# Top-1 routing behind windowed attention: rows kept in token order, and a table of row numbers built by one-hot matmuls

## The chip, the cores and the metric

The kernel runs on one core of a Trainium2 chip. The metric is device time in microseconds (us) for one execution of the whole program. Beside the times there is one profiled execution, which tells for every engine (PE the matrix engine, PEld its weight loads, DVE the vector engine, ACT the scalar engine, POOL the general engine, SP the one that only issues transfers) what ran when and what ended each wait.

## The reference

Two stages run one behind the other. The first is attention over 8 batches, 8 heads, 576 positions of 64 numbers, in which a query sees the positions within 32 of its own and 8 global positions, and a global query sees all. The second sends each of the 4608 tokens (512 numbers) to one of 8 experts, the one with the largest gate logit, and scales that expert's answer by its softmax weight.

```python
mask = np.abs(pos[:, None] - pos[None, :]) <= 32
mask = mask | is_global[:, None] | is_global[None, :]
attn = softmax(where(mask, q @ k.T / 8, -1e9))
x = (attn @ v).transpose(0, 2, 1, 3).reshape(4608, 512)

logits = x @ w_gate
expert_idx = np.argmax(logits, axis=1)
gate_w = softmax(logits)[arange, expert_idx]
for e in range(8):
    m = expert_idx == e
    out[m] = gate_w[m, None] * (np.maximum(x[m] @ w1[e], 0) @ w2[e])
```

The inputs are drawn once and fixed. The experts get 446, 387, 871, 515, 596, 674, 404 and 715 tokens.

## The kernel before

**Layout.** `wall` holds the weights of all experts in f16 (16 KB of each partition for one expert). Until the weights of experts 2 to 7 arrive, their place is carved up for attention: q and k in f32 and f16, v for two batches (`vb`), exponentials for two steps (`eb`), four staging buffers, and `x16b[0]`, the finished rows of even batches. `x16b[1]`, for odd batches, is a tile of the attention pool. A row is ROW = 516 words of 16 bits: 512 numbers in f16, the token number (32 bits) and the softmax weight (f32).

**The loop.** The outer loop runs over the 8 batches, the inner one over t, 6 steps a batch. A step computes the scores of the next step (`scores`, L419), their exponentials on ACT (`exps`, L443), then `pvs` (L447, 32 matmuls) and `zs` (L461, the sums of the exponentials, 32 matmuls) of its own, and adds them into `xt` and `zt` (`merge`, ACT L486 and DVE L491). Every engine works through its instructions in the order in which the code writes them; nothing reorders them. `man = tc.manual_schedule()` (L158) fixes that order for all but the last part.

At the head of a batch SP is told to load v of the next batch and q, k of the one after that (L800 to L807), POOL casts q and k (L328), and `sum_globals` adds what belongs to the global positions. `join` at the end of a batch runs on POOL.

**Routing.** `Tail(b)` (L521) follows a batch. Its steps are spread over the batch behind it, and a last few over the one behind that, where it is called `done`. `gate` and `logits` compute the gate logits, `route1` the one-hot expert choice, `ranks` counts with small matmuls how many tokens of the same expert stand before each token, and `route2` (L637) makes of it `si`, the number of the token's slot: expert times CAP (4608) plus its rank. `rows` (L574) transposes the attention result and writes it, divided by its sums, to `x16`; `exps` (L619) writes token numbers there and `weights` (L654) the softmax weights. `scatter` (L661) then sends 108 rows at a time to their slots of the DRAM scratch `xslot`, by indirect DMA from POOL, one per step t of the batch after:

```python
d_ = nc.gpsimd.indirect_dma_start(
    out=xslot, out_offset=IndirectOffsetOnAxis(ap=self.si[p, j : j + 1], axis=0),
    in_=self.x16[p, j, :].bitcast(I16), in_offset=None, ...)
```

With 6 scatters for each of 8 batches and one for the global positions there are 49.

**The wave.** Experts 0 and 1 start early. When five batches have been scattered, `wave_plan` (L745, called in batch 6 at t = 0) tells how many of their first 256 slots are filled, and four gathers in batch 7 (L925) fetch these rows. `wave` (L763) computes both experts on them, cut into 24 pieces of PE work that `waves(n)` inserts between the last routing steps. All of the rest (the routing of batch 7, called `tail`, that of the global positions, called `tg`) stands behind the loop, L940 to L999.

**The experts.** `gathers(e)` (L1021) fetches 128 rows at a time from consecutive slots, two experts ahead. The wait of the first gather covers all scatters. For each expert there are 8 blocks of `h` matmuls (L1155), a relu into `ht`, and `yp` matmuls (L1176); `yout` scales by the softmax weight and scatters to the output (L720). In between, f32 pieces of the later experts' weights are loaded by SP into five staging tiles (`wload`, L675) and cast by ACT or DVE (L684, L686). An expert handles at most 512 slots here. What is over goes to blocks of 128 in a list: `overflow_plan` (L1082), computed on DVE while expert 2 runs, makes for each of up to NOV blocks its expert and row numbers; `chain` (L1237) runs them three at a time.

Of the kernel before, what the change touches and what calls it, by code (L numbers as in the profile page):

```python
# [41 lines left out]
NOV = 33  # L42
# [3 lines left out]
def kernel(  # L46
# [14 lines left out]
    xslot = nc.dram_tensor("xslot_scr", (E * CAP, ROW), I16, kind="Internal").ap()  # L61
# [39 lines left out]
    x16b = [carve(TB, 6 * ROW, FP16).rearrange("p (j n) -> p j n", j=6)]  # L101
# [9 lines left out]
    x16b.append(ap_.tile([TB, 6, ROW], FP16, name="x16x"))  # L111
# [43 lines left out]
    ofs = sb.tile([128, 4], FP32, name="ofs")  # L155
    gif4 = gidw.rearrange("p (g w) -> p g w", w=2)
# [148 lines left out]

    eqs = short(NSL, NG)
# [77 lines left out]
    def routing_constants():  # L384
# [12 lines left out]
        nc.vector.tensor_copy(revr, ri)  # L397
        up = ap_.tile([TB, 1], FP32, name="up")
# [119 lines left out]
    scattered = []  # L518


    class Tail:  # L521
        def __init__(self, b):
            self.b = b
            self.glob = b == B
            self.nj = 1 if self.glob else 6
            self.np = 64 if self.glob else TB
            self.lg = ap2.tile([TB, 6, 8], FP32, tag="lg", name="lg")
            self.rz = ap2.tile([TB, 6, 8], FP32, tag="rz", name="rz")
            self.x16 = x16b[b % 2]
            self.lsb = {}  # L530

# [105 lines left out]
        def route2(self):  # L637
# [10 lines left out]
            self.si = ap2.tile([TB, 6], I32, tag="si", name="si")  # L648
            if self.glob:
                nc.vector.tensor_copy(self.si[p, 0:J], sl[p, 0:J])  # L650
            else:
                nc.vector.tensor_tensor(out=self.si, in0=sl, in1=invbig, op=ALU.add)
# [8 lines left out]
        def scatter(self, js=None):  # L661
            p = slice(0, self.np)
            for j in range(self.nj) if js is None else js:
                d_ = nc.gpsimd.indirect_dma_start(  # L664
                    out=xslot, out_offset=IndirectOffsetOnAxis(ap=self.si[p, j : j + 1], axis=0),
                    in_=self.x16[p, j, :].bitcast(I16), in_offset=None,
                    bounds_check=E * CAP - 1, oob_is_err=False)
                tc.declare_no_dep(d_.ins, group="xslot", reason="every token has a slot of its own")
                tc.add_to_no_dep_group("xslot", d_.ins)
                scattered.append(d_.ins)  # L670
# [17 lines left out]
    def gather(xr, ix, behind=None):  # L688

        nc.gpsimd.memset(xr[:, DM : DM + 2].bitcast(I32), 10 ** 6)  # L690
        d_ = nc.gpsimd.indirect_dma_start(out=xr.bitcast(I16), out_offset=None, in_=xslot,  # L691
                                          in_offset=IndirectOffsetOnAxis(ap=ix, axis=0),
                                          bounds_check=E * CAP - 1, oob_is_err=False)
        if behind is not None:
            tc.declare_no_dep(d_.ins, group="xslot", keep=behind, reason="reads slots of those alone")
            tc.add_to_no_dep_group("xslot", d_.ins)
            return
        while scattered:
            tc.add_manual_dep(d_.ins, scattered.pop().name, mybir.DependencyInfo(
                mybir.DependencyClass.Sync, mybir.DependencyReason.DATA), reason="slots of all tokens")  # L700
# [37 lines left out]
    idw = sb.tile([128, NW, 2], FP32, name="idw")  # L738
    wi = sb.tile([128, NW, 2], I32, name="wi")
    st = sb.tile([128, E], FP32, name="st")  # L740
    idre = sb.tile([128, E, 4], FP32, name="idre")
    ofsb = ofs.rearrange("p (o j) -> p o j", o=1)
    ebb = ebasef.rearrange("p (e o) -> p e o", o=1)

    def wave_plan():  # L745

        bw = sb.tile([128, NW], FP32, name="bw")
        nc.vector.scalar_tensor_tensor(out=bw, in0=base[(B - 3) % 2][:, 0:NW], scalar=-1.0, in1=ebasef[:, 0:NW],
                                       op0=ALU.add, op1=ALU.max)
        nc.vector.tensor_tensor(out=idw, in0=ofsb[:, :, 0:2].to_broadcast([128, NW, 2]),  # L750
                                in1=ebb[:, 0:NW].to_broadcast([128, NW, 2]), op=ALU.add)
        w_ = sb.tile([128, NW, 2], FP32, name="w_")
        nc.vector.tensor_tensor(out=w_, in0=idw, in1=bw.rearrange("p (e o) -> p e o", o=1).to_broadcast([128, NW, 2]),
                                op=ALU.is_ge)
        nc.vector.scalar_tensor_tensor(out=wi, in0=w_, scalar=BIG, in1=idw, op0=ALU.mult, op1=ALU.add)

        nc.vector.memset(st, 0.0)
        nc.vector.tensor_tensor(out=st[:, 0:NW], in0=bw, in1=ebasef[:, 0:NW], op=ALU.subtract)
        nc.vector.tensor_single_scalar(out=st[:, 0:NW], in_=st[:, 0:NW], scalar=float(HALF), op=ALU.min)
        nc.vector.tensor_tensor(out=idre, in0=ofsb.to_broadcast([128, E, 4]), in1=ebb.to_broadcast([128, E, 4]), op=ALU.add)  # L760
        nc.vector.tensor_tensor(out=idre, in0=idre, in1=st.rearrange("p (e o) -> p e o", o=1).to_broadcast([128, E, 4]), op=ALU.add)
# [36 lines left out]
    for b in range(B):  # L798
        if b + 1 < B:
# [10 lines left out]
        if b + 1 == B:  # L810
            for x_ in xr01:
                nc.gpsimd.memset(x_, 0.0)
        for t in range(NT):
# [108 lines left out]
            if b + 2 == B and t == 0:  # L922
                wave_plan()
# [365 lines left out]
```

## Time and profile before

| what | value |
|---|---|
| median of 14 runs | 512.09 us (505.01 to 515.59) |
| the profiled execution's own time | 510.35 us |
| its span | 508.6 us |
| granted PE clock, mean of the span | 0.908 |
| busy: PE, PEld, DVE, ACT, POOL | 414.4, 255.0, 254.1, 211.5, 241.2 us |
| DMA, 84.06 MB | mean 165 GB/s |
| of it by SP's queue; by POOL's queue | 63.57 MB; 19.38 MB |
| instructions of PE | 6661 matmuls, as many weight loads |

By stage, from the busy times of stretches:

| stretch (us) | what runs | PE busy | DVE busy | POOL busy |
|---|---|---|---|---|
| 0 to 299.9 | eight batches | 243.32 | 158.66 | 136.03 |
| 300 to 319.6 | last routing, with the wave's pieces | 14.60 | 14.39 | 11.42 |
| 319.6 to 336 | the rest of the wave | 11.66 | 0.33 | 8.81 |
| 337 to 372 | experts 0, 1 and 2 | 26.84 | 25.44 | 19.63 |
| 372 to 422 | experts 3 to 7 | 49.76 | 26.53 | 29.52 |
| 422 to 508.6 | overflow blocks, last outputs | 67.92 | 27.75 | 35.58 |

A row of a group reads: line, engine, operation, output tile <- input tiles, shapes, how often; then busy time and the mean length of one in ns; then the idle time of the engine just before these instructions and what ended most of it. "issue" stands for a wait that ended with nothing the profile shows, "remote" for one that an update of unknown origin ended.

### The profile page before, as it was taken

How to read it: one execution, taken by the hardware profiler on the slowest of the kernel's cores; microseconds unless marked ns; L12 is line 12 of the kernel's file. 1: busy time of each engine (PE TensorE's matmuls, PEld its weight loads, DVE VectorE, ACT ScalarE, POOL GpSimd, SP SyncE). 2: the span in 40 equal slices, each digit the busy share in tenths (PEclk: the TensorE clock that was granted, in tenths of full speed). 3: DMA queues.
4: the chain of work that ended last, by engine and by line, in shares of the span. 5: the costliest groups of instructions: out<-in, count | busy, mean ns of one | idle time of the engine just before them, and what ended most of it. 6: DMA issues, size and time to landing. Idle time of an engine off the chain costs nothing.

```text
span 508.6 us, 16371 instructions
## 1 busy us (share of the span) xinstructions
PE 414.4 (81%) x6661; PEld 255.0 (50%) x6661; DVE 254.1 (50%) x719; ACT 211.5 (42%) x385; POOL 241.2 (47%) x387
## 2 busy tenths in 40 slices
PE   3777789988799799795996777687699999999980
PEld 2455557656476476473663544355344444444440
DVE  7525356635276366375573447145865555333330
ACT  6234444533245245372571552243535444223330
POOL 7700371836607508347057234655545655543441
PEclk9998998978879789698698789699999999999996
DMA  8696979864925728857243201579989999221011
GB/s 204 105 208 112 211 155 207 189 146 96 216 49 119 198 49 184 270 124 190 71 159 112 66 21 54 160 249 337 341 278 366 363 357 319 84 75 66 20 33 49
DMA packets 119436, 84.06 MB, mean 165 GB/s; under 512 B 46552, under 2 KB 113880, under 8 KB 119356
## 3 DMA queue, kind: packets, MB, share of 16 engines
q1 hardware_dynamic: 110300, 63.57, 49.3%
q0 software_dynamic: 9056, 19.38, 11.6%
q8 instruction: 55, 0.90, 0.8%
q14 instruction: 25, 0.20, 0.1%
HBM read 68.51 MB, written 16.16 MB: 166 GB/s over the span
## 4 chain that ended last, share of the span: by engine, by line
PE 23%; issue 10%; DMA 8%; POOL 5%; DVE 5%; ACT 3%; POOLq 1%; SPq 0%; another core or an unknown queue 0%; DVEq 0%; ACTq 0%
PE yp L1176 5%; PE h L1155 4%; DMA st<-in_moe_w_dram 4%; DMA xr<-xslot_scr,ovi 3%; PE pv L456 3%; POOL xr L691 3%; POOL out_dram L720 2%; PE z L468 2%; PE hp L769 2%; PE tr_x L580 2%; PE yw L776 1%; ACT wall L684 1%; PE tx L706 1%; DVE xt L491 1%; ACT xt L486 1%
## 5 line engine op out<-in xcount | busy, mean ns | idle before, releaser
L456 PE MATMUL pv<-wall 56*64 56x128 f32 x1536 | 80.8, 314 | 15.3 <-issue 14.3
L456 PEld LDWEIGHTS pv<-wall 56*64 56x64 f32 x1536 | 57.4, 155 | 34.3 <-issue 30.6
L445 ACT ACTIVATE wall<-sc 128x1024 f32<-128x1024 f32 x48 | 49.1, 1023 | 58.8 <-remote 40.9
L491 DVE TENSOR_TENSOR xt<-xt,pv 128x288 f32<-128x288 f32 x80 | 36.3, 454 | 59.9 <-ACT xt L486 47.8
L486 ACT ACTIVATE xt<-pv 128x224 f32<-128x224 f32 x96 | 34.3, 357 | 73.6 <-PE pv L456 28.3
L506 POOL TENSOR_TENSOR xt<-xt 128x144 f32<-128x144 f32 x14 | 7.1, 509 | 121.3 <-DVE xt L491 121.3
L1155 PE MATMUL h<-xts,wall 128*128 128x512 f16 (+1 forms) x256 | 53.5, 352 | 5.8 <-ACT ht L735 3.5
L1176 PE MATMUL yp<-wall,ht 128*128 128x512 f16 x224 | 50.3, 379 | 1.8 <-DVE ht L733 0.9
L468 PE MATMUL z<-wall,onesel 56*32 56x128 f32 x1536 | 45.1, 304 | 7.2 <-issue 6.8
L720 POOL DMA_INDIRECT out_dram<-y,xr x24 | 25.1, 1045 | 38.2 <-DVE y L717 23.6
L328 POOL CAST wall<-wall 96x768 f16<-96x768 f32 (+1 forms) x48 | 37.4, 822 | 3.2 <-DMA wall<-in_v_dram 3.2
L1155 PEld LDWEIGHTS <-wall 128*128 128x128 f16 x256 | 24.2, 98 | 26.7 <-issue 6.2
L684 ACT ACTIVATE wall<-st 128x1024 f16<-128x1024 f32 x24 | 25.3, 1054 | 26.1 <-DMA st<-in_moe_w_dram 24.0
L580 PE MATMUL tr_x<-id,xt 128*108 128x128 f32 x192 | 32.8, 301 | 4.0 <-DVE x16x L581 1.8
L468 PEld LDWEIGHTS z<-wall,onesel 56*32 56x32 f32 x1536 | 24.0, 115 | 22.0 <-issue 18.5
L1176 PEld LDWEIGHTS <-ht 128*128 128x128 f16 x224 | 21.3, 98 | 27.4 <-DVE ht L733 2.4
L664 POOL DMA_INDIRECT xslot_scr<-wall,si x25 | 24.9, 995 | 17.8 <-ACT wall L445 9.1
L438 PEld LDWEIGHTS <-kt 64*64 64x64 f16 x1536 | 27.7, 121 | 7.8 <-issue 4.3
L733 DVE TENSOR_SCALAR ht<-h 128x512 f16<-128x512 f32 (+1 forms) x32 | 19.9, 623 | 23.2 <-PE h L1155 17.5
L664 POOL DMA_INDIRECT xslot_scr<-x16x,si x24 | 24.0, 999 | 12.4 <-issue 10.8
L691 POOL DMA_INDIRECT xr<-xslot_scr,idx x24 | 25.0, 1040 | 8.6 <-POOL xr L690 4.5
L341 PE MATMUL tr_qk<-idh,wall 96*128 96x96 f16 x192 | 16.3, 231 | 15.6 <-DVE wall L328 7.2
(270 smaller groups left out, 749.2 us busy)
## 6 DMA issues: line engine op xcount, KB each, us to landing
st<-in_moe_w_dram SPq DMA_DIRECT2D x96, 256.0 KB
wall<-in_v_dram SPq DMA_DIRECT2D x96, 96.0 KB
wall<-in_moe_w_dram SPq DMA_DIRECT2D x32, 256.0 KB
wall<-in_k_dram SPq DMA_DIRECT2D x42, 192.0 KB
wall<-in_q_dram SPq DMA_DIRECT2D x42, 192.0 KB
wall<-vg SPq DMA_DIRECT2D x14, 96.0 KB
wall<-in_k_dram SPq DMA_DIRECT2D x4, 288.0 KB
wall<-in_q_dram SPq DMA_DIRECT2D x4, 288.0 KB
```

The lines of the kernel that those rows point to most:

```text
L328: eng.tensor_copy(o, i_)
L445: nc.scalar.activation(out=e.rearrange("p r c w -> p r (c w)"), in_=sc[:, :, 0 : 4 * WE], func=AF.Exp, scale=0.125)
L456: nc.tensor.matmul(out=pv[64 * r : 64 * r + 64, f, c * WE : (c + 1) * WE], lhsT=vt[ff, t, 64 * h : 64 * h + 64], rhs=e[ff, r, c, :], start ...
L468: nc.tensor.matmul(out=z[32 * c : 32 * c + 32, f, 0:WE], lhsT=onesel[ff, r, :], rhs=e[ff, r, c, :], start=(r == 0), stop=(r == 1))
L486: nc.scalar.activation(out=new[i][0], in_=new[i][1], func=AF.Copy)
L491: nc.vector.tensor_tensor(out=d_, in0=d_, in1=s_, op=ALU.add)
L580: nc.tensor.transpose(out=ps[p, 128 * c : 128 * c + 128], in_=src, identity=id32)
L664: d_ = nc.gpsimd.indirect_dma_start(out=xslot, out_offset=IndirectOffsetOnAxis(ap=self.si[p, j : j + 1], axis=0), in_=self.x16[p, j, :].bi ...
L691: d_ = nc.gpsimd.indirect_dma_start(out=xr.bitcast(I16), out_offset=None, in_=xslot, in_offset=IndirectOffsetOnAxis(ap=ix, axis=0), bounds ...
L720: d_ = nc.gpsimd.indirect_dma_start(out=out, out_offset=IndirectOffsetOnAxis(ap=xr[:, DM : DM + 2].bitcast(I32), axis=0), in_=y, in_offset ...
L1155: nc.tensor.matmul(out=ps, lhsT=w1v[:, e, c, 128 * fb : 128 * fb + 128], rhs=xts[:, c, 0:N], start=(c == 0), stop=(c == 3))
L1176: nc.tensor.matmul(out=ps, lhsT=ht[:, fc, 128 * j : 128 * j + 128], rhs=w2v[:, e, fc, :], start=(fc == 0), stop=(fc == 7))
```

## The change

The scratch in DRAM is now `xrow`, in the order of tokens: row 128 x (6b + j) + p for partition p of column j of batch b. `store` writes x16 there by a plain transfer that SP issues: columns 0 to 4 of `done` at the head of a batch, column 5 at t = 1, and those of the last three `Tail`s behind the loop. No scatter is left but those to the output.

Where a slot's row lies is now computed. `acc` (128 partitions x 8 experts x 36 columns) has a place for every slot: slot number modulo 128 is the partition, expert and slot / 128 the column. For 108 tokens `hot` makes three f16 one-hots: of the slot's lower 7 bits (128 wide), and two of its column (8 x n wide, n growing from 5 to 36 with the batch), one times 128 x (6b + j + 1), the other times p. `slots` multiplies the first with the other two on PE, for two to four columns j at a time, and DVE adds the product to `acc`. An entry is the row number plus 128, or 0 where no token is. `row_of` makes of it the index of a gather, and a large number where the entry is below 64. In the loop POOL makes the one-hots; behind it POOL and DVE share them.

x16 is a single buffer for batches 0 to 5 and 7; batch 6 and the globals use the place of v of the even batches. Because slots that the wave took are found by a snapshot of `acc`, partly taken blocks of experts 0 and 1 become overflow blocks (NOV is 39 instead of 33), and `overflow_plan` finds its columns of `acc` by transposes, selections and matmuls.

```diff
-    xslot = nc.dram_tensor("xslot_scr", (E * CAP, ROW), I16, kind="Internal").ap()
+    xrow = nc.dram_tensor("xrow_scr", (NROW, ROW), I16, kind="Internal").ap()
...
-    x16b = [carve(TB, 6 * ROW, FP16).rearrange("p (j n) -> p j n", j=6)]
+    x16b = [carve(TB, 6 * ROW, FP16).rearrange("p (j n) -> p j n", j=6)] * B
+    v16 = vb[B % 2].rearrange("p t n -> p (t n)").bitcast(FP16)[0:TB]
+    x16b[B - 2] = v16[:, 0 : 6 * ROW].rearrange("p (j n) -> p j n", j=6)
+    x16b.append(v16[:, 6 * ROW : 7 * ROW].rearrange("p (j n) -> p j n", j=1))
-    x16b.append(ap_.tile([TB, 6, ROW], FP16, name="x16x"))
...
+            nc.vector.tensor_single_scalar(out=lo[p, 0:J], in_=si[p, 0:J], scalar=127, op=ALU.bitwise_and)
+            nc.vector.tensor_copy(self.low[p, 0:J], lo[p, 0:J])
+            nc.vector.tensor_tensor(out=self.chk[p, 0:J], in0=si[p, 0:J], in1=self.low[p, 0:J], op=ALU.subtract)
...
-        def scatter(self, js=None):
...
+        def store(self, j0, j1):
+            p = slice(0, self.np)
+            r0 = 128 * (6 * self.b + j0)
+            d_ = nc.sync.dma_start(
+                out=xrow[r0 : r0 + 128 * (j1 - j0)].rearrange("(j p) n -> p j n", p=128)[p],
+                in_=self.x16[p, j0:j1, :].bitcast(I16))
...
+        def hot(self, j, eng):
+            p = slice(0, self.np)
+            h = hots[len(taken) % 4]
+            taken.append(h)
+            n = min(NCH, -(-S * (self.b + 1) // 128))
...
+            eng.tensor_scalar(out=h[0][p], in0=iop[p], scalar1=self.low[p, j : j + 1], scalar2=None, op0=ALU.is_equal)
+            for o, v_ in ((h[1], 128.0 * (6 * self.b + j + 1)), (h[2], pos1[p])):
+                eng.tensor_scalar(out=o[p, 0 : E * n].rearrange("p (e n) -> p e n", e=E), in0=io,
+                                  scalar1=self.chk[p, j : j + 1], scalar2=v_, op0=ALU.is_equal, op1=ALU.mult)
+        def slots(self):
...
+            for i, (l, o) in enumerate(hs):
+                nc.tensor.matmul(out=ps[:, 0 : E * n], lhsT=l[p], rhs=o[p, 0 : E * n], start=(i == 0), stop=(i + 1 == len(hs)))
+            av = acc.rearrange("p (e n) -> p e n", e=E)[:, :, 0:n]
+            nc.vector.tensor_tensor(out=av, in0=av, in1=ps[:, 0 : E * n].rearrange("p (e n) -> p e n", e=E), op=ALU.add)
...
+    def row_of(dst, v_, t_):
+        nc.vector.tensor_scalar(out=t_, in0=v_, scalar1=64.0, scalar2=BIG, op0=ALU.is_lt, op1=ALU.mult)
+        nc.vector.scalar_tensor_tensor(out=dst, in0=v_, scalar=-128.0, in1=t_, op0=ALU.add, op1=ALU.add)
...
     for b in range(B):
+        if done is not None:
+            done.store(0, 5)
         if b + 1 < B:
             load_v(b + 1)
...
+            wave_plan()
...
-            if b + 2 == B and t == 0:
-                wave_plan()
...
             if done is not None:
-                done.scatter([t])
-            if b + 1 == B and t >= 4:
-                tail.scatter([t - 4])
+                if t == 1:
+                    done.store(5, 6)
+                    for j in range(4):
+                        done.hot(j, nc.gpsimd)
+                elif t >= 4:
+                    done.slots()
+                    if t == 4:
+                        for j in (4, 5):
+                            done.hot(j, nc.gpsimd)
...
-    done.scatter([2, 3, 4, 5])
+    done.store(0, 6)
+    for j in range(4):
+        done.hot(j, nc.gpsimd)
...
     tail.exps()
-    waves(2)
+    done.slots()
+    for j in (4, 5):
+        done.hot(j, nc.gpsimd)
+    waves(1)
     tail.rows(0, 0)
     waves(1)
     tail.ranks()
     tail.route2()
-    tail.weights()
-    tail.rows(0, 1)
+    done.slots()
+    for j in (4, 0, 1):
+        tail.hot(j, nc.vector if j < 4 else nc.gpsimd)
     tg.gate(0)
     waves(1)
-    tail.rows(1, 0)
     tg.logits(0)
     tg.route1()
     tg.exps()
-    tail.rows(1, 1)
-    waves(1)
+    tail.slots()
+    for j in (5, 2, 3):
+        tail.hot(j, nc.vector if j < 4 else nc.gpsimd)
     tg.ranks()
     tg.route2()
+    waves(1)
+    tail.slots()
+    tg.hot(0, nc.vector)
+    tail.weights()
     tg.weights()
+    tail.rows(0, 1)
+    tail.rows(1, 0)
+    tg.slots()
+    nc.vector.tensor_tensor(out=acv[:, 0:NW, 0:2], in0=acv[:, 0:NW, 0:2], in1=snap, op=ALU.subtract)
...
+    row_of(idx, acv[:, :, 0:4], idf)
+    tail.rows(1, 1)
     tail.rows(2, 0)
     waves(1)
     tail.rows(2, 1)
     tg.rows(0, 0)
+    tail.store(0, 6)
+    tg.store(0, 1)
     waves(99)
-    tail.scatter()
-    tg.scatter()
...
+        for i_ in range(3):
+            nc.tensor.transpose(out=ps[0:96, 128 * i_ : 128 * i_ + 128], in_=acc[:, 96 * i_ : 96 * i_ + 96], identity=id32)
+        nc.vector.tensor_copy(acct.rearrange("p a b -> p (a b)"), ps[0:96, 0:384])
...
+            nc.vector.tensor_scalar(out=sel[:, i_, :], in0=ovs[0:96], scalar1=colp[:, i_ : i_ + 1], scalar2=None, op0=ALU.is_equal)
...
+            nc.tensor.matmul(out=ps[:, 0:NOV], lhsT=acct[:, i_, :], rhs=sel[:, i_, :], start=(i_ == 0), stop=(i_ == 2))
+        row_of(ovi, ps[:, 0:NOV], lt)
```

## The prediction

> **What bounds the kernel now.** I read the page first (groups and chain), then the busy times of stretches, then the order of time inside one batch.
>
> ```profile
> PE 23%; issue 10%; DMA 8%; POOL 5%; DVE 5%; ACT 3%; POOLq 1%; SPq 0%; another core or an unknown queue 0%; DVEq 0%; ACTq 0%
> L664 POOL DMA_INDIRECT xslot_scr<-wall,si x25 | 24.9, 995 | 17.8 <-ACT wall L445 9.1
> L664 POOL DMA_INDIRECT xslot_scr<-x16x,si x24 | 24.0, 999 | 12.4 <-issue 10.8
> ```
>
> The chain lists PE and then 10% of "issue", time in which an engine waited for nothing that shows. The 49 scatters cost POOL 1.0 us each, and POOL is busy only 47% of the span, so by busy time alone their removal would be worth nothing. Where the "issue" lies, the stretches tell (length; busy time and instructions of PE, PEld, DVE, ACT, POOL; granted clock; DMA share; GB/s):
>
> ```profile
> core 0: us, PE busy (x) PEld busy (x) DVE busy (x) ACT busy (x) POOL busy (x), PEclk, DMA share, GB/s
> 100.00:108.50 8.50, 5.51 (x40) 2.96 (x41) 1.14 (x3) 0.94 (x2) 4.98 (x5) 0.75 1.06 241
> 124.80:131.90 7.10, 6.80 (x210) 4.46 (x206) 4.50 (x13) 3.93 (x8) 5.98 (x13) 1.00 1.06 249
> 131.90:140.00 8.10, 5.05 (x35) 2.37 (x34) 0.59 (x3) 1.02 (x1) 4.97 (x5) 0.69 0.81 193
> 140.00:158.30 18.30, 18.04 (x480) 13.58 (x487) 12.92 (x39) 9.51 (x21) 2.17 (x6) 0.86 0.25 52
> 169.50:177.50 8.00, 4.67 (x36) 2.88 (x37) 0.69 (x1) 1.19 (x2) 4.42 (x5) 0.69 0.80 197
> 202.50:211.00 8.50, 5.23 (x38) 2.53 (x36) 0.90 (x2) 1.38 (x2) 4.89 (x5) 0.74 1.12 326
> 236.50:245.00 8.50, 5.73 (x66) 2.90 (x58) 2.14 (x7) 2.15 (x5) 4.54 (x5) 0.70 0.64 191
> 270.00:283.00 13.00, 8.67 (x94) 3.74 (x93) 2.80 (x7) 2.89 (x7) 8.26 (x11) 0.69 0.34 102
> ```
>
> Once in each of the batches 2 to 7, PE runs 35 to 94 matmuls where 124.8 to 131.9 has 210 in 7.1 us (29 a us). DVE and ACT almost stop too. It is no lack of DMA: 124.8 to 131.9 has a share of 1.06 and full speed, 270 to 283 has 0.34 and none. What every slow stretch has is POOL issuing indirect DMAs back to back:
>
> ```profile
> 131.99 0.45 PE L456 MATMUL pv<-wall 56*64 56x128 f32 x5
> 132.13 1.00 POOL L664 DMA_INDIRECT xslot_scr<-x16x,si  x1 [0.30 <-issue]
> 132.82 0.44 PE L456 MATMUL pv<-wall 56*64 56x128 f32 x4 [0.38 <-issue]
> 137.99 1.02 ACT L445 ACTIVATE wall<-sc 128x1024 f32<-128x1024 f32 x1 [6.42 <-remote]
> 144.97 1.18 PE L456 MATMUL pv<-wall 56*64 56x128 f32 x32
> ```
>
> The 32 matmuls that take 1.18 us at 144.97 trickle out in fours from 131.99 to 139.9 while six scatters issue (130.8 to 138.3), and the exponential, whose scores were done at 131.6, starts at 137.99. Batch 1 has no scatters, but four gathers on POOL (70.7 to 75.7), and fours of matmuls from 73.5 to 76.5. From 302 to 308 four scatters beside thin matmul work show no trickle: it takes dense matmuls.
>
> **The change, part by part** (against the profiled run, 510.35 us; the median of the 14 runs is 512.09, 1.7 more).
>
> *Scatters gone from the loop.* At 29 matmuls a us the six stretches would need 40/29 = 1.4, 1.2, 1.2, 1.3, 2.3 and 3.2 us. Recovered: 7.1 + 6.9 + 6.8 + 7.2 + 6.2 = 34.2, and in batch 7, where four of the ten indirect DMAs are gathers that stay, six tenths of 9.8 = 5.9. Together -40.1; bounds 0 (the trickle has another cause) and -44 (the gathers alone harm little). The clock stays low behind each stretch (0.86 over 140 to 158.3, 26 matmuls a us); at 28 a us that stretch and its four likes save some 1 us each: -5 (0 to -8).
>
> A rule weighs against this term. The row is the trickle, 35 matmuls in 8.1 us. The Trainium skill, "SBUF — State Buffer", section "Who interferes with whom", says that PE and ACT never wait on anyone and that a DMA contends with no compute engine; "DMA: Bandwidth & Descriptors", section "Issuing engines are not separate DMA queues", that DMAs of every issuing engine run on the same 16 engines and another issuer saves only sequencer time. By these the scatters can't be the cause and the total would be that of the first rival below; by the row it is the forecast. The row decides.
>
> *Slot matmuls on PE.* Twelve a batch, 108x128 against 40 to 216 columns, six batches in the loop. Six f16 transposes of 128 columns took 0.51 us at 146.08, 0.08 each: 12 x 0.08 x 6 = +6 (0 in gaps of PE; +14 at 0.2 each, the single 128x56 matmul of L630). They take a turn in the two-buffer PSUM pool, freed by a DVE add of 40 to 216 columns (0.45 for 288 at L491): +0.5 a batch, +3 (0 to 6). The three new small DVE operations of route2 (0.17 each, L652) lie in DVE's idle time (12.92 of 18.3 busy): 0; at worst 0.5 a batch, inside that bound.
>
> *One-hots on POOL.* 18 a batch, 128 or 40 to 216 elements. A 128x384 copy takes 0.50, a 128x192 sum 0.59, so 0.3 each: 5.4 us for the 7.8 that six scatters hold POOL. POOL idles 13 to 18 us a batch before its join (L506 waits 121.3 us in 7): 0. It can touch DVE, though, as this row shows, two columns beside POOL's casts:
>
> ```profile
> 226.87 1.69 DVE L748 SCALAR_TENSOR_TENSOR bw<-base,ebasef 128x2 f32<-128x2 f32 x1
> ```
>
> The casts are longer (0.82) than a one-hot, and the DVE operations met are a few of route1: inside the +3.
>
> *Stores on SP.* store(0,5) heads each batch and waits for weights(), so the loads that ran ahead during the previous batch now start behind it. A set of loads takes SP 21.6 us where nothing holds it (57.87 to 79.44); batch 3 lasts 33.5 us and would last about 27. The loads fit, cover for v and q/k is kept. store(5,6), behind them, lands some 23 us into the batch; exps() (L623) then writes the same single x16 buffer at about 19 (26.4 in the trace less 7.5) and holds ACT 4 us. PE has 3.9 us of work that needs no ACT (scores 0.8, pv 1.1, z 0.7, two rows 1.3). I take 1.5 in batches 2 to 5: +6 (0 to 18).
>
> *wave_plan* moves from batch 6, where DVE spends 226.9 to 232.3 on it and PE is busy 7.28 of 226 to 236.5, to the start of batch 7, shorter and without casts beside it: -3 (0 to -3).
>
> *After the loop.*
>
> ```profile
> 300.00:319.60 19.60, 14.60 (x124) 9.20 (x124) 14.39 (x56) 5.68 (x16) 11.42 (x17) 1.00 0.16 45
> 319.60:336.00 16.40, 11.66 (x51) 5.89 (x51) 0.33 (x2) 3.54 (x9) 8.81 (x13) 0.69 0.74 231
> 358.70:372.20 13.50, 8.14 (x44) 3.49 (x43) 12.97 (x45) 4.85 (x6) 5.42 (x9) 1.00 0.99 317
> 372.00:422.00 50.00, 49.76 (x267) 23.89 (x266) 26.53 (x46) 24.64 (x32) 29.52 (x39) 1.00 1.04 348
> ```
>
> 300 to 319.6 is a chain between DVE and PE. On DVE it gains five adds of 0.45, five one-hots (0.2 for 128 columns, two of 0.35 for 288, between 0.18 for 33 and 0.43 for 264) of 0.9, six operations of 0.17 and 0.5 of row numbers that must precede the gathers: 2.3 + 4.5 + 1.0 + 0.5 = 8.3. PE adds 26 matmuls in five bursts, about a third of a us each on the chain. +10 (3 if the wave's matmuls cover it, 16 if POOL's one-hots, due before the first slots(), come late). Everything behind is pushed: waves(99), the first FFN expert. The weight fetch (322.8 before, behind the scatters) starts behind the last store, about 329, still ahead of the first cast by more than its five buffers need (ten issues in 6.73 us): 0, up to 6.7 without that cover. The first gathers hide under the 16 us of waves(99): 0, 3 without. The scatters' gaps on PE here (1.10 and 1.56 at 319.65 and 321.80): -2.5.
>
> *Overflow plan.* In expert 2 DVE is the bound, 12.97 of 13.5. Added: nine small operations (1.5), two more later (0.3), three selections (0.6), a PSUM copy (0.5), row_of (0.4), 39 for 33 columns on ten of 0.43 (0.8): 4.1, with PE's transposes about +5 (0 if the weights would be late anyway, 8). Behind it PE is full (49.76 of 50), so nothing wins it back.
>
> **Sum:** -40.1 - 5 + 6 + 3 + 6 - 3 + 10 - 2.5 + 5 = -20.6; 510.35 - 20.6 = 489.8, and 1.7 more for the median: **491**.
>
> **Rivals.**
> 1. *The trickle belongs to the rows' traffic, not to POOL's issuing.* The same 648 rows of 1032 bytes a batch are still written. For: all six stretches have rows in flight. Against: batch 1 trickles beside gathers, and 270 to 283 at a share of 0.34. Then -40.1, -5 and -2.5 fall away: 510.35 + 27 + 1.7 = 539. It decides from the point where less than 27 of those 47.6 us come back.
> 2. *SP's queue becomes the loop's bound.* 21.6 us of loads, some 4 for 0.66 MB of rows at the loads' rate, then a block until weights(): ACT's wait reaches PE, 4.5 a batch instead of 1.5: +12, 503. For: one x16 buffer instead of two. Against: 26 still fits in 27.
> 3. *Added work hides and the clock comes back whole.* For: DVE and ACT idle in much of the loop. Against: PE is busy 6.80 of 7.10. Slot matmuls 0, clock -8, PSUM turns 3, ACT's wait 3, after the loop 3: 510.35 - 40.1 - 8 + 3 + 3 - 3 + 3 - 2.5 + 5 + 1.7 = 472.
>
> **Chances.** Forecast 0.56, rival 1 0.16, rival 2 0.14, rival 3 0.10, and 0.04 that the terms cancel. The likeliest case by itself: 480 to 502. The range reaches over rivals 2 and 3 and leaves rival 1 out: 472 to 513. A measurement of this kernel tells about 0.5%, 2.5 us, from no change: faster 0.80, same 0.04, slower 0.16.
>
> **What would show it.** Right: no stretch of 8 us with fewer than 60 matmuls in batches 2 to 6, a short one beside the four gathers of batch 7, batches of 27 to 29 us, the loop ending near 267 instead of 300. Store step: idle time of ACT before L623 put down to a DMA, below 4 us a batch. Tail: last rows() about 29 us behind the loop instead of 19. Plan: expert 2 some 5 us longer. Wrong if the fours of matmuls reappear while the stores run, or if DVE's or POOL's rows show the one-hots at over 1 us each.

## The result, and the profile after

The changed kernel takes 521.57 us (median of 10 runs, 519.13 to 523.02), the kernel before in the same measurement 512.14 (47 runs, 503.6 to 521.19): a ratio of 1.026 [1.023, 1.029]. The forecast was 491. The profiled execution takes 519.77 with a span of 517.9, 9.4 more than the one before.

One sentence is needed to read any other number: of six series of runs (five on one chip each; for this one the record names no chip) the kernel before took 503 to 521 us in two (this one among them) and 446 to 460 in four, so times are compared only within a series, and a ratio is that of the fast runs of both kernels in one series.

The stages, by the first or last instruction of each (length of the stage in us; the lower pair is from experiments on one chip of the other kind):

| kernel | loop, to its last pv | to the last rows() | to h of expert 0 | experts 0 to 2 | experts 3 to 6 | expert 7 to the last output scatter | to the end |
|---|---|---|---|---|---|---|---|
| before | 297.5 | 21.7 | 17.8 | 39.7 | 60.4 | 65.7 | 5.8 |
| after | 277.8 | 38.2 | 14.3 | 51.1 | 59.9 | 66.4 | 10.2 |
| before, other chip | 244.8 | 21.1 | 12.6 | 38.8 | 62.4 | 63.6 | 5.8 |
| after, other chip | 267.8 | 39.0 | 14.1 | 46.0 | 58.9 | 66.1 | 10.2 |

The loop did get shorter, by 19.7, and the stages from there to the end of expert 2 gave back 24.4, the last one 4.4. The page of the kernel after, chain and groups:

```profile
PE 35%; POOL 15%; issue 13%; DMA 12%; DVE 9%; SPq 7%; ACT 4%; another core or an unknown queue 1%; POOLq 1%; ACTq 0%; DVEq 0%
L710 POOL TENSOR_SCALAR hot<-ioc,chk,pos 108x40 f16<-108x40 f16 (+7 forms) x44 | 38.5, 875 | 3.8
L708 POOL TENSOR_SCALAR hot<-iop,low 108x128 f16<-108x128 f16 x44 | 26.8, 608 | 23.4 <-PE tr_s L720 23.3
```

POOL's share of the chain went from 5% to 15% although 49 scatters of 1.0 us left it: one-hots cost 0.61 to 0.88 us on average, and SP's queue, 0% before, holds 7%.

The busy times of four stretches of the kernel after (columns as in the prediction):

```profile
108.50:114.30 5.80, 1.72 (x65) 1.26 (x64) 0.00 (x0) 0.07 (x1) 0.59 (x2) 0.95 0.74 148
199.10:206.00 6.90, 0.61 (x33) 0.34 (x32) 0.00 (x0) 0.12 (x1) 0.00 (x0) 0.74 1.16 271
281.00:295.50 14.50, 7.05 (x59) 3.96 (x59) 5.34 (x20) 2.58 (x8) 13.42 (x19) 0.85 0.00 0
332.00:338.20 6.20, 0.69 (x10) 0.53 (x8) 0.85 (x2) 0.79 (x2) 5.09 (x13) 0.79 0.66 199
```

Each has its own cause. In the first two POOL does next to nothing (0.59 and 0.00 us), so it isn't the trickle of before; the order of time shows what ACT waits for:

```profile
108.57 10.85 SPq L692 DMA_DIRECT2D xrow_scr<-wall  x2
114.23 0.21 ACT L644 ACTIVATE wall<-tokt 108x6 int32<-108x6 int32 x1 [8.26 <-DMA xrow_scr<-wall]
144.40 0.21 ACT L644 ACTIVATE wall<-tokt 108x6 int32<-108x6 int32 x1 [2.97 <-issue]
173.85 0.21 ACT L644 ACTIVATE wall<-tokt 108x6 int32<-108x6 int32 x1 [4.98 <-DMA xrow_scr<-wall]
205.88 1.06 ACT L736 ACTIVATE wall<-wall 128x1024 f16<-128x1024 f32 x1 [9.79 <-DMA wall<-in_moe_w_dram]
```

SP issues store(5,6) at 108.57, behind twelve loads of q and k; its data land at 114.1, and `exps` (L644), which overwrites the one x16 buffer, waits 8.26. In batch 5 it is the cast of a weight (L736) that waits 9.79, for a load which SP issues behind the same queue.

In the third stretch, behind the loop, POOL is busy 13.42 of 14.5:

```profile
288.77 0.61 POOL L708 TENSOR_SCALAR hot<-iop,low 108x128 f16<-108x128 f16 x1
289.47 1.15 POOL L710 TENSOR_SCALAR hot<-ioc,chk 108x256 f16<-108x256 f16 x1
290.67 0.27 PE L720 MATMUL tr_s<-hot,hot 108*128 108x256 f16 x1 [1.55 <-POOL hot L710]
```

Three one-hots a column take POOL 3.1 us, and a slot matmul waits behind each.

In the fourth four gathers (L743) go out while expert 0 begins:

```profile
332.95 1.08 POOL L743 DMA_INDIRECT xr<-xrow_scr,idx  x1 [0.27 <-POOL xr L742]
337.22 1.00 POOL L743 DMA_INDIRECT xr<-xrow_scr,idx  x1 [0.27 <-POOL xr L742]
337.74 0.38 ACT L788 ACTIVATE ht<-h 128x256 f16<-128x256 f32 x1 [5.33 <-remote]
338.18 3.57 PE L1268 MATMUL h<-xts,wall 128*128 128x256 f16 x16 [5.51 <-ACT ht L788]
```

The matmuls that ACT's relu waits for are short and had long run. The trace has the moment at which each engine's semaphore counter moves. PE's moves 0.015 us (the median) after the end of a matmul group. Here:

```
end of PE's group:      330.90  331.34  331.57  332.00  332.44
PE's counter moves at:  330.92  334.06  336.26  337.72  339.17
gathers issued on POOL at:      332.95, 334.43, 335.83, 337.22
```

By these times the work was done (the profile models the ends of matmuls), and the news of it came one step per indirect DMA. The kernel before shows the same beside the scatters of the loop: a group that ended at 131.54 moves the counter at 137.91, and the exponential of the prediction's row starts at 137.99; the largest delay is 7.3 us. The four scatters from 302.8 to 306.7 delay nothing by more than 0.4. So ACT's long waits in the trickle are late semaphores while POOL issues indirect DMAs back to back. The matmuls in fours are not explained by that: the groups from 132.82 on wait for no semaphore in the trace and still start 0.7 to 1.4 us apart. What holds them and the counters up together stays open.

### The profile page after: what moved, and what is told of

Read it like the earlier page. It is cut to its first block, busy times and chain, and to the rows that moved or that the text cites. A ratio compares the mean times of both kernels' runs of the same rounds, so it can differ in the third digit from the quotient of the medians.

```text
span 517.9 us, 16684 instructions
## 1 busy us (share of the span) xinstructions
PE 406.3 (78%) x6768; PEld 256.0 (49%) x6768; DVE 266.2 (51%) x793; ACT 210.6 (41%) x385; POOL 293.9 (57%) x474
## 4 chain that ended last, share of the span: by engine, by line
PE 35%; POOL 15%; issue 13%; DMA 12%; DVE 9%; SPq 7%; ACT 4%; another core or an unknown queue 1%; POOLq 1%; ACTq 0%; DVEq 0%
PE pv L476 7%; PE h L1268 5%; PE yp L1289 4%; SPq L180 4%; POOL hot L710 4%; DMA xr<-xrow_scr,ovi 3%; PE tr_x L601 3%; POOL xr L743 3%; PE z L488 3%; DMA out_dram<-y,xr 3%; POOL out_dram L773 3%; SPq L189 3%; POOL wall L342 2%; DMA wall<-in_moe_w_dram 2%; DMA xrow_scr<-wall 2%
## 5 line engine op out<-in xcount | busy, mean ns | idle before, releaser
L476 PE MATMUL pv<-wall 56*64 56x128 f32 x1536 | 65.7, 308 | 2.1 <-issue 0.8
L1268 PE MATMUL h<-xts,wall 128*128 128x512 f16 (+1 forms) x256 | 56.5, 369 | 11.2 <-ACT ht L788 10.6
L465 ACT ACTIVATE wall<-sc 128x1024 f32<-128x1024 f32 x48 | 49.1, 1023 | 32.8 <-PE sc L458 22.4
L476 PEld LDWEIGHTS pv<-wall 56*64 56x64 f32 x1536 | 51.6, 152 | 11.9 <-issue 4.8
L602 DVE TENSOR_TENSOR wall<-tr_x,rz 108x512 f16<-108x512 f32 (+1 forms) x49 | 33.3, 686 | 25.6 <-ACT wall L644 13.0
L1268 PEld LDWEIGHTS <-wall 128*128 128x128 f16 x256 | 25.2, 102 | 33.6 <-issue 13.7
L710 POOL TENSOR_SCALAR hot<-ioc,chk,pos 108x40 f16<-108x40 f16 (+7 forms) x44 | 38.5, 875 | 3.8
L708 POOL TENSOR_SCALAR hot<-iop,low 108x128 f16<-108x128 f16 x44 | 26.8, 608 | 23.4 <-PE tr_s L720 23.3
L710 POOL TENSOR_SCALAR hot<-ioc,chk 108x40 f16<-108x40 f16 (+7 forms) x44 | 35.5, 807 | 3.3
L488 PE MATMUL z<-wall,onesel 56*32 56x128 f32 x1536 | 36.2, 296 | 1.4 <-issue 1.4
L601 PEld LDWEIGHTS tr_x<-id,xt 128*108 128x108 f32 x192 | 21.9, 144 | 29.4 <-DVE wall L602 15.3
L1289 PEld LDWEIGHTS <-ht 128*128 128x128 f16 x224 | 22.4, 102 | 26.9 <-issue 3.2
L743 POOL DMA_INDIRECT xr<-xrow_scr,idx x24 | 26.1, 1087 | 7.5 <-issue 3.8
L736 ACT ACTIVATE wall<-st 128x1024 f16<-128x1024 f32 x24 | 25.2, 1052 | 12.3 <-issue 9.3
```

The source lines that it names most:

```text
L465: nc.scalar.activation(out=e.rearrange("p r c w -> p r (c w)"), in_=sc[:, :, 0 : 4 * WE], func=AF.Exp, scale=0.125)
L476: nc.tensor.matmul(out=pv[64 * r : 64 * r + 64, f, c * WE : (c + 1) * WE], lhsT=vt[ff, t, 64 * h : 64 * h + 64], rhs=e[ff, r, c, :], start ...
L488: nc.tensor.matmul(out=z[32 * c : 32 * c + 32, f, 0:WE], lhsT=onesel[ff, r, :], rhs=e[ff, r, c, :], start=(r == 0), stop=(r == 1))
L601: nc.tensor.transpose(out=ps[p, 128 * c : 128 * c + 128], in_=src, identity=id32)
L710: eng.tensor_scalar(out=o[p, 0 : E * n].rearrange("p (e n) -> p e n", e=E), in0=io, scalar1=self.chk[p, j : j + 1], scalar2=v_, op0=ALU.is ...
L1268: nc.tensor.matmul(out=ps, lhsT=w1v[:, e, c, 128 * fb : 128 * fb + 128], rhs=xts[:, c, 0:N], start=(c == 0), stop=(c == 3))
```

## The experiments

The theory: (A) the removal pays what the trickle cost, and is overtaken by ACT's waits for late stores, one-hots on POOL, and a longer plan; (B) the rival: the rows' traffic, or the plain stores themselves, keep the engines waiting whatever their order.

**1. Store ahead of the loads.**

```diff
-                load_qk(b + 2) if b + 2 < B else None
+                if b + 2 < B and done is None:
+                    load_qk(b + 2)
...
                 if t == 1:
                     done.store(5, 6)
+                    if b + 2 < B:
+                        load_qk(b + 2)
```

> The changed kernel with one move: the q/k loads of the batch after next are issued behind store(5,6), not ahead of it, so that the last row of the single x16 buffer no longer waits for twelve loads on SP's queue. Theory (the loop falls short of the forecast because store(5,6) lands late): the idle time of ACT before its token write (13.2 us put down to the DMA, 3.0 to issue) and before the first weight cast (9.8) goes, the loop ends 12 to 20 us earlier, and the total is 502 to 510 instead of 521.6. Rival (the loads had no slack): POOL's casts and PE's transposes of q and k wait instead, and the total stays within 4 us of 521.6.

Measured: 496.21 against 452.95 for the kernel before, 1.105 [1.094, 1.116]. Idle time of ACT before L644, in this kernel and then in the changed kernel as it was, run on another chip of the same kind (experiment 6):

```profile
  DVE wall L602: 5.9, 6
```

```profile
  DMA xrow_scr<-wall: 10.9, 2
  DVE wall L602: 3.2, 3
  issue: 2.6, 1
```

The waits for a store are gone. The loop takes 260.4 us against 269.8 in experiment 2, which has the changed kernel's loop and ran on the same chip: -9.4, less than expected. What moved is the issue of store(5,6): 10.0 to 10.5 us behind store(0,5) instead of 20.1 to 20.5. From its issue to the last of its landings the store takes 5.0 to 5.3 us here and took 4.1 to 5.6 in the changed kernel, so the loads ahead of it cost SP's time to issue them, and no more on the way. What is left of the queue's cost is the cast of the weights, which still waits 8.6 (12.3 as it was). And the kernel before, at 453 us here, was the first sign of two kinds of chips.

**2. One-hots of batch 6 behind the loop on DVE.** `done.hot(j, nc.gpsimd)` becomes `done.hot(j, nc.vector)` in the two places behind the loop, 18 one-hots.

> The changed kernel with the eighteen one-hots of batch 6, issued behind the loop, on DVE instead of POOL. Theory (the stretch behind the loop grew by 16 us because POOL takes 0.61, 1.15 and 1.22 us for one-hots that DVE does in 0.24 to 0.44): PE's waits before the slot matmuls there go, the last rows() end some 9 us earlier, total 510 to 514. Rival (DVE is that stretch's own chain, and 18 more operations of 0.3 fill it): gain of less than 3 us, total 518 to 522.

Measured: 500.52, 1.115 [1.103, 1.126]. From the loop's end to the last rows() 29.9 us against 38.3 in experiment 1: -8.4. The same one-hots on DVE:

```profile
281.89 0.25 DVE L708 TENSOR_SCALAR hot<-iop,low 108x128 f16<-108x128 f16 x1
282.05 0.28 DVE L710 TENSOR_SCALAR hot<-ioc,chk 108x256 f16<-108x256 f16 x1
282.25 0.34 DVE L710 TENSOR_SCALAR hot<-ioc,chk,pos 108x256 f16<-108x256 f16 x1
```

0.25, 0.28 and 0.34 where POOL takes 0.61, 1.15 and 1.22. The stage is then 29.9 - 21.1 = 8.8 longer than before's, close to the +10 of the prediction, which had taken POOL's one-hots at 0.3.

**3 and 4. Scatters put back beside the stores**, one a step into a scratch of their own, with rows of 8 bytes (3) or 1032 (4). Nothing reads them.

```diff
+            d_ = nc.gpsimd.indirect_dma_start(
+                out=xdum, out_offset=IndirectOffsetOnAxis(ap=self.si[p, j : j + 1], axis=0),
+                in_=iop[p, 0:4].bitcast(I16), in_offset=None, ...)
```

> The changed kernel with one indirect scatter a slice added in batches 2 to 7, on POOL, as the kernel before had it, but of 8 bytes a row from a constant tile into a spare tensor: the issues without the traffic. Theory (POOL's issuing holds the other engines up): stretches with fours of matmuls and ACT idle put down to remote come back, 4 to 7 us in each of the six batches, in part in place of the waits for the stores; total 536 to 560. Rival (the rows' bytes did it): no such stretch, total within 4 us of 521.6.

> As the tiny scatters, but 1032 bytes a row, the full row's size, from a constant tile into a spare tensor, beside the plain stores. Theory (issuing): within 5 us of the run with tiny scatters. Rival (bytes): at least 15 us above it.

Measured, once each: 538.07 and 524.03. The first lies in the range of the theory (536 to 560), but without its mark. The short rows cost more than the long ones, which no theory expected, and both loops (306.3 and 290.4) are far longer than the 260 to 270 of the others. No run of a few matmuls beside the scatters appears on this chip; what grows are ACT's waits before its token write, mostly for the store (29.9 and 21.4 us before L645 in all, 16.7 for the same write in experiment 6, without scatters). So the two don't tell issuing from bytes where it matters.

**5 and 6. The two kernels once more, on one chip**, nothing changed.

> The kernel before, unchanged, profiled beside the others: in the four runs so far it took 447 to 457 us, where the runs behind the prediction had 503 to 521. Theory (the stretches of fours belong to some chips or days and not to the scatters as such): in this profile no stretch of 8 us has fewer than 60 matmuls in batches 2 to 6, the loop ends near 250 and no ACT wait before the exponentials is put down to remote. Rival (the stretches are there and something else is 60 us shorter): they show at the scatters as before.

> The changed kernel, unchanged, on the same chip as the two before it. Theory (what the change adds costs the same everywhere, what it removes exists only where the stretches of fours do): about 508, the run with the one-hots on DVE (500.5) and 8 more, so some 55 us slower than the kernel before here, while it was 2.6% slower where the stretches were. Rival (the changed kernel loses as much as the kernel before has gained): near 460.

Measured: before 450.83 (450.95 over the series), after 511.67, 1.144 [1.133, 1.154]. These stretches are of the kernel before on this chip, each holding six scatters:

```profile
94.40:102.10 7.70, 7.61 (x235) 5.75 (x234) 6.16 (x19) 4.88 (x11) 6.04 (x6) 1.00 1.11 267
120.00:127.70 7.70, 7.12 (x227) 5.12 (x219) 5.75 (x18) 4.45 (x10) 5.97 (x6) 1.00 1.16 242
```

And the same kernel on a chip of the first kind, the one of 503 to 521 us (experiment 11):

```profile
106.00:113.70 7.70, 5.04 (x68) 2.54 (x60) 1.02 (x4) 0.97 (x2) 6.00 (x6) 0.87 1.14 249
138.00:145.60 7.60, 4.98 (x73) 2.55 (x62) 1.71 (x6) 1.39 (x2) 5.96 (x6) 0.79 1.04 228
```

Same six scatters, POOL busy the same 6 us, same traffic: 227 to 235 matmuls on one chip, 68 to 73 on the other. The late counter tells the two kinds apart too: in none of the 12 traces from chips of 446 to 460 us does PE's counter move more than 1 us after the last group that had ended, in the five others it does so 13 to 29 times. On the chips of 446 to 460 us there is nothing to remove. There the loop shows what the change adds by itself: 267.8 - 244.8 = +23.0.

**7. Both moves together**, and the one-hots of batch 7 on DVE too.

```diff
-                        done.hot(j, nc.gpsimd)
+                        done.hot(j, nc.gpsimd if b + 1 < B else nc.vector)
```

> The changed kernel with both moves (q/k loads behind store(5,6), the one-hots behind the loop on DVE) and the one-hots of batch 7 on DVE too, so that the wave's gathers do not stand behind 18 one-hots on POOL. Theory: the gains add, 10 for the loads, 8 for the one-hots, 4 for the gathers: 22 below the unchanged one of this call. Rival (DVE is full in batch 7: 8.4 of 10 us in places): the last part gives nothing or costs up to 5.

Measured: 492.11 (488.72 to 494.57), 1.094 [1.084, 1.105]; the changed kernel took 503.99 to 515.92 on the same chip, so by the shortest runs the gain is 15.3, short of the 22. The loop took 266.5, more than the 260.4 of experiment 1, but 4.6 of that arise before batch 6, where the two kernels are alike. From there on it is 1.4 longer: the twelve one-hots on DVE, in a batch where DVE serves PE's sums, save nothing.

**8. Before, with each scatter replaced by a plain store.**

```diff
-                d_ = nc.gpsimd.indirect_dma_start(
-                    out=xslot, out_offset=IndirectOffsetOnAxis(ap=self.si[p, j : j + 1], axis=0),
...
+                r0 = 108 * (6 * self.b + j)
+                d_ = nc.sync.dma_start(out=xslot[r0 : r0 + self.np], in_=self.x16[p, j, :].bitcast(I16))
```

It leaves out the table of row numbers, so the gathers fetch rows of other tokens; the slots' capacity is cut to 640.

> The kernel before with each scatter replaced by one plain store of the same 108 rows from SP, in token order, and nothing of the one-hots, slot matmuls or plan; the expert slots count from bases 640 rows apart, so the gathers fetch rows of the wrong tokens, in the same number. This is the removal and the stores without the rest. Theory (here the scatters hold nobody up): the loop ends at 245 plus or minus 3, as in the kernel before of the last call, and the total is 447 to 455. If this chip has the stretches of fours (the kernel before at 503 or more): the loop ends 40 earlier than in the kernel before. Rival (the scatters cost the loop something on every chip): loop 8 or more earlier than 245, total below 442.

Measured: 460.38 against 454.28, 1.027 [1.013, 1.041], on a chip of the second kind: a miss, for 447 to 455 were expected. The profiled run, the longest of the four with 466.24, has a loop of 253.9 instead of 245 (3.2 of it from before the first store) and takes 10.5 us from the last output scatter to the end, where the kernel before takes 5.8. Replacing the scatters alone, without one-hots or slot matmuls, gains nothing there; it costs 2.7%, 1.3 to 4.1 by the interval.

**9. The order mended:** experiment 7, with the loads of batch 5 later, and the one-hots of batch 7 one column a step.

```diff
+                if b + 1 == B:
+                    if t in (3, 5):
+                        done.slots()
+                    for j in ((0,), (1,), (2,), (3,), (4, 5), ())[t]:
+                        done.hot(j, nc.vector)
+                elif t == 3 and b == 5:
+                    load_qk(b + 2)
```

> The changed kernel with the q/k loads behind store(5,6), in batch 5 also behind the first three loads of expert weights, the one-hots behind the loop on DVE, and those of batch 7 on DVE one a slice, so that the wave's gathers find POOL free. Theory (the loop's loss over the kernel before, 23 us, is waits by order and not the added work): no ACT wait over 3 us for a DMA in the loop, batches of 27 to 30 us, the loop ends 12 to 18 us earlier than 267.8, total 474 to 484 (unchanged: 504 to 516). Rival (slot matmuls and one-hots themselves fill the loop): ends later than 260.

Measured: 486.82, 1.088 [1.070, 1.107], a miss: the loop is 258.2, not below 256. The weights' cast still waits 7.3 us, in two places. But with no store in ACT's way, the time from the token write of one `Tail` (`exps`, L644) to that of the next (us, batches in order) tells what the matmuls and one-hots cost:

| kernel | batches 2 to 5 | sum | 6, 7 |
|---|---|---|---|
| before (experiment 5) | 24.7 28.1 27.5 28.5 | 108.8 | 29.1 17.1 |
| after (experiment 6) | 30.5 30.2 29.6 37.5 | 127.8 | 30.4 22.5 |
| store early (experiment 1) | 25.0 29.1 27.1 28.3 | 109.5 | 36.7 19.7 |
| order mended (experiment 9) | 25.2 30.4 28.6 28.3 | 112.5 | 34.4 22.7 |

Experiment 1 has all slot matmuls, their PSUM turns and all of POOL's one-hots in these four batches and needs 0.7 us more than before; experiment 9 needs 3.7 more, and experiment 7, alike there, 4.1. In batches 6 and 7 experiments 1 and 9 take 10.2 and 10.9 more than before; the waits for weights are part of it, the rest isn't taken apart.

**10. The plan spread over experts 2 and 3**, on top of experiment 9, three steps a block instead of four.

```diff
-        plan = iter(overflow_plan()) if e == 2 else iter(())
+        plan = iter(overflow_plan()) if e == 2 else plan if e == 3 else iter(())
...
-        for _ in plan:
+        for _ in plan if e != 2 else ():
```

> The kernel of the mended order with the overflow plan spread over experts 2 and 3, three steps a block of h instead of four and none flushed at the end of expert 2. Theory (the plan's added DVE work, on the path in expert 2, is the +5 of the sum, and takes 7): expert 2 is 4 to 7 us shorter (from its first h to that of expert 3: 28.3 in the mended kernel), expert 3 at most 1 longer, total 478 to 484. Rival (late weights set expert 2 anyway): less than 1.5 us gained.

Measured: 493.93 (492.08 to 497.84) against 516.06: 0.963 [0.953, 0.973], on a chip of the first kind. It beats both kernels there. Expert 2 in experiment 9 (a chip of the second kind) and then here:

```profile
321.60:349.90 28.30, 19.72 (x91) 9.59 (x90) 19.01 (x66) 8.60 (x11) 9.61 (x13) 0.82 0.75 262
```

```profile
337.10:356.30 19.20, 15.09 (x81) 7.05 (x80) 16.86 (x53) 7.54 (x10) 10.26 (x14) 1.00 0.98 338
```

Against experiment 12, on the same chip, expert 2 falls from 26.0 to 19.2, and expert 3 grows from 15.4 to 16.6: some 5.6 net.

**11 and 12. Before and after on that chip**, nothing changed.

> The kernel before, unchanged, for the stages on this chip. On a chip without the stretches of fours: 447 to 459, loop end 245 plus or minus 5. With them: 503 to 521, loop end near 297.

> The changed kernel, unchanged, for the stages on this chip. On a chip without the stretches: 500 to 516, loop end 268 plus or minus 4, the same waits of ACT before its token write and its first weight cast. With them: 518 to 523, loop end near 278.

Measured: 517.57 and 523.74, one run each. The change costs 6.2 us here and 9.4 in the prediction's measurement, the same direction, with one run each on a chip where seven runs of the kernel before spread from 510.41 to 520.22. The idle time of ACT before its exponentials in the kernel before has the mark of this kind of chip:

```profile
  remote: 38.8, 6
  PE sc L438: 16.7, 21
```

38.8 us in six waits that end with an update the profile can't place; the changed kernel has one such wait there, 5.1 us, in the prediction's trace, and the kernel before none in experiment 5.

**13. Gathers of expert 2 behind expert 0's matmuls**, on top of experiment 10; **14 and 15** are experiments 3 and 4 unchanged. All three were to run where the semaphores are late.

> The kernel with the spread plan, with the four gathers for expert 2 issued behind the blocks of h of expert 0 instead of ahead of them. On a chip with the stretches of fours (the kernel before at 503 or more): theory (POOL's back-to-back issues hold ACT, DVE and PE up) expert 0, 16.3 us from its first h to that of expert 1, falls to 9 to 12, total 488 to 493. Rival (the wait there is for weights): expert 0 stays within 1.5 us of 16.3. On a chip without them (447 to 459): expert 0 at 8 in any case, total 478 to 486.

> The changed kernel with the 36 scatters of 8 bytes a row, once more. On a chip with the stretches: theory (issuing) matmuls in fours and ACT waits put down to remote come back beside the scatters in batches 2 to 7, which the changed kernel has there in none of batches 2 to 6, total 545 to 575. Rival (bytes): none comes back, total 536 to 545 as on a chip without them plus the 8 us that POOL's gathers cost there. On a chip without them: 530 to 540 again.

> The changed kernel with the 36 scatters of 1032 bytes a row, once more. On a chip with the stretches: theory (issuing) the same stretches as with 8 bytes, within 1.5 us each. Rival (bytes): stretches here and none with 8 bytes. On a chip without them: 518 to 528 again, below the run with 8 bytes.

The chip was of the second kind: 487.35, 1.080 [1.074, 1.086], then 542.60 and 518.68. Experiment 13 had no stall to remove: experts 0 and 1 took 9.0 and 14.1 us, where experiment 9, with the gathers ahead, took 7.8 and 10.9. What it does where the semaphores are late stays open. The other two repeat that 8-byte rows cost more than long ones.

## Why the prediction was wrong

**Scatters gone, clock: right in size, on this kind of chip.** The forecast was -40.1 - 5. The loop changed by -19.7 here and by +23.0 where there is no trickle; if the added work costs the same on both, the removal is worth -19.7 - 23.0 = -42.7 (experiments 11 and 12: 280.5 - 304.8 - 23.0 = -47.3). Up to the token write of batch 1, ahead of the first store, one-hot and slot matmul, the runs already differ by up to 6.7 us; counted from there the +23.0 is +27.1 and the removal -45.9 and -44.7. That the added work does cost the same is supported by the same four batches as in the table: after takes 128.2 on the prediction's chip and 127.8 on the other, before 135.8 and 108.8. The trickle didn't come back while the plain stores ran, and the stores carry the same bytes, so rival 1 falls for this kernel. What was wrong is that the term was taken as a property of the kernel. It is one of the kernel on a chip: experiments 5, 6 and 8 show none of it.

The rule weighed in the prediction comes out differently by chip. The Trainium skill, "SBUF — State Buffer", section "Who interferes with whom", has PE and ACT wait on no one; 227 to 235 matmuls beside six scatters agree with it, 68 to 73 do not. The section speaks of ports of the SBUF; the delays here are in the moving of counters and in the start of matmuls that wait for no semaphore, and of these it says nothing.

**Stores on SP: the step that failed most.** It took "+6 (0 to 18)", with ACT held 4 us a batch and 1.5 of it reaching PE. The hold came out as forecast: 8.26, 2.97 and 4.98 us in batches 2 to 4, and none in batch 5, where the cast's 9.79 comes first: 16.2 in four batches. What failed is the overlap, 1.5 of 4: in experiments 2 and 1, on one chip, the earlier store takes away 15.3 us of these waits, and the batches 2 to 7 become 14.8 shorter (180.7 to 165.9), so nearly all of the hold had reached the loop. And the prediction never asked what else stands in that queue: the weights for experts 0 and 1, whose cast had waited 0.0 us in the loop before and now waits 12.0; idle time of ACT before these casts (L736) in the changed kernel:

```profile
  DMA wall<-in_moe_w_dram: 12.0, 2
```

By size, in experiment 6 against experiment 5, stores (10.9 + 2.6) and weights (12.3 against 3.4) make 22.4 of the +23.0; by experiment only the store's part is shown, and 9.4 of it came back in the loop (experiment 1), since 4.0 were lost again behind the last token write and 1.5 ahead of the first. The weights' part is argued: no run took their wait away. Rival 2 had this step nearly right: 4.5 a batch make 18 instead of 6, the loop's additions +24 instead of +12, against +23.0. Its total of 503 missed what lies behind the loop.

**Slot matmuls, PSUM turns, DVE's small operations: +9 forecast for six batches, 0.7 to 4.1 shown in four** (experiments 1, 9 and 7); in batches 6 and 7 they aren't told from the waits for weights. With wave_plan's -3, the loop's added terms were +12 and measured +23.0.

**After the loop: +10 forecast, +16.5 here and +17.9 on the other chip.** The mechanism was right (DVE and PE in a chain). The price of a one-hot was not: 0.3 was read off a copy and a sum, and POOL took 0.61 for 128 columns and 1.15 and 1.22 for 256, over the 1 us that it had named as a sign of being wrong. The prediction's upper end, "16 if POOL's one-hots come late", is what happened; experiment 2 puts them on DVE and comes to +8.8. The Trainium skill, "GPSIMD Engine Reference", section "3.1 Elementwise — side-by-side cycle accounting", gives 1.96 times DVE's time for an add of 2048 fp32 elements; the ratios here, for another operation on short f16 rows, are 0.61/0.25 = 2.4 and 1.15/0.28 = 4.1, so for these the measurement decides.

**Overflow plan: +5 forecast; +7.2 over experts 0 to 2 on the other chip, +11.4 here.** The direction held (experiment 10 takes 5.6 of it back), and its bound of 8 too. The 4.2 more on this chip go with the late semaphores beside the first gathers, PE waiting 5.51 at 338.18: expert 0 takes 15.1 us here, 7.8 before and 7.8 on the other chip, and expert 1 gives 2.8 back. The gathers moved from under the wave to the first expert, which the prediction priced at "0, 3 without".

**The end: nothing forecast, +4.4 measured.** From the last output scatter to the end 10.2 us instead of 5.8, the same in every kernel of the changed kind. POOL's closing wait lasts 9.5 us in the kernels that issue 101 indirect DMAs on POOL, 5.2 in those with 150, 4.4 in those with 137 (experiments 3, 4, 14 and 15). Experiment 8, which only replaces the scatters and so issues 101, has it too: it comes with the scatters' removal, not with one-hots or plan. Why stays open.

Made up, with +23.0 for the loop's additions: against the forecast, the removal missed 2.4 us, the loop's additions 11, the stage behind it 6.5, the way to expert 0 -1.0, the first experts 6.4, the end 4.4, the rest 0.2: 29.9. Forecast -20.6, measured +9.4, 30.0 apart. No single term turned the sign; the store step is the largest.

## What to carry to other kernels

A transfer put into a queue is priced by when its turn comes behind the transfers that are issued ahead of it (here 20 us behind the head of the batch, or 10) and by its own time to landing (4 to 6 us), and everything else that waits in the same queue is priced with it. That an engine has other work doesn't say that the work fits into the wait: here nearly all of ACT's hold reached the loop. Elementwise work moved to POOL is priced from a row of the same shape on POOL, or, going by the rows here, taken as 2.4 to 4.1 times DVE's. A cost that shows as idle engines without a shared buffer may belong to the chip and not to the kernel: measure it on a second chip before building on its removal.

## What was not expected of the hardware

- Two kinds of chips: the same kernel takes 450.83 us on one and 517.57 on another, steady within a series. Whether it is the chip or a state that it was in isn't known.
- On the slower kind, while POOL issues indirect DMAs back to back (one each 1.3 to 1.5 us), PE's semaphore counter moves up to 7.6 us after the work has ended (experiment 11); the median is 0.015 us. Matmuls that wait for no semaphore start late as well. Plain stores from SP with the same bytes do nothing of the kind. Whether 8-byte scatters would wasn't shown: both tries met the other kind.
- 36 scatters of 8-byte rows made the kernel slower than 36 of 1032 bytes: 538.07 and 542.60 against 524.03 and 518.68. The Trainium skill, "DMA: Bandwidth & Descriptors", section "Specifications", says that transfers below 512 bytes are done as a read and a write back; the direction agrees, and no run here isolates it.
